# A batch's q and k through the DMA's transposition, and a new order of loads, in a fused attention and MLP kernel

## The chip, the cores and the metric

The kernel runs on one core of a Trainium2 chip. What counts is the device time of one execution in microseconds (us). Before the change the median of three runs is 226.33 us (226.27 to 227.69); the profiled execution spans 224.6 us, with TensorE's granted clock at 0.998.

A core has engines with an instruction queue each, worked off in order: TensorE (PE, matmuls; its weight loads are shown as PEld), VectorE (DVE), ScalarE (ACT), GpSimd (POOL) and SyncE (SP), which here only issues transfers. Transfers run on 16 DMA engines. Engines wait for each other, and for transfers, through semaphores. An instruction that waits holds back all that stand behind it on its engine.

## What is computed

Attention over a sliding window of 128 keys and four "sink" keys that all queries see, for 4 batches, 8 heads, 768 tokens and head size 64; then a layer norm and a two-layer MLP with a residual, on rows of 512:

```python
keep = (pos[None, :] < 4) | ((rel >= 0) & (rel < 128))        # rel = query - key
a = softmax(where(keep, q @ k.T / 8, -1e9))
x = (a @ v), heads side by side                                # (4, 768, 512)
xn = (x - mean) / sqrt(var + 1e-6) * g_ln
out = x + relu(xn @ w_ch1) @ w_ch2                             # 512 -> 2048 -> 512
```

Inputs and output are float32 in HBM; the matmuls run in bfloat16, and the loads issued by GpSimd change the type on the way.

## The kernel before

**Tiles.** A tile is 128 tokens of one batch: 24 tiles, six a batch (`RB`). For each tile `scores` (L545) multiplies k's block with 256 queries (its own and the next tile's) and takes the exponential on ScalarE; `values` (L617) multiplies with v, divides, takes the layer norm's statistics, and turns the normed rows so that the MLP can use them, on PE for tiles 0 to 9 and by a DMA transposition on SyncE from tile 10 (`DMA_TILE`). `sinks` handles the four sink keys of a batch and needs all its q blocks from token 256 on.

**MLP.** `up` (L731) computes hidden units of a group of tiles, `down` (L768) four of the sixteen hidden blocks (a "quarter") of one tile's output; the fourth quarter is followed by the residual and the store on SyncE. `GROUPS` is [2, 2, 2, 4, 4, 4, 4, 2]: the first three groups (`NB0`) are batch 0. Weights w1 and w2 come in four pieces of 512 KB (in bfloat16) each. `up` needs the piece of w1 for its hidden blocks, `down` the piece of w2 for its quarter; in the kernel before, quarters 0 and 1 wait for piece 2 (`w_in[(2, max(quarter, 2))]`).

**q and k.** Scores need q and k with the head dimension in the partitions. Three ways lead there. Batch 0 and batch 1 are loaded in long runs (`load_runs`, L346): batch 0 in two chunks of 384 tokens (the first four heads of chunk 0 by `load_first`), batch 1 whole, 768 KB each for q and k; `prep_runs` (L434) then turns them with PE transpositions (L454) and copies them out of PSUM on DVE and ACT (L222/L224). Batches 2 and 3 are loaded by token blocks of 128 KB (`load_qk`, L387), and `prep` (L470) turns each block with one DMA transposition issued by SyncE. `CHUNKS` tells which batches go which way.

**What sets the order.** Nothing is issued in the order in which the Python code calls it. Each piece of work is an `Op` with a cost for each engine that can do it, its dependencies and a due key; `Plan.emit` (L57) runs a list schedule over these and emits the instructions in the resulting order, one list for each engine. Costs and latencies are constants in the code: `LAT` by engine, the `took` of a load on one serial "DMA" resource, and for a DMA transposition an issue of 1.25 us on SP, 0.4 on a resource of its own ("XD") and 6.0 of extra latency (L481, L710). Up to `WARM` (26 us of the plan) the planner fills PE's gaps with `spin` matmuls (L236) of no use to the result. `HOLD` sets until when an operation of lower key may be taken ahead of a more urgent one's start. PSUM is two double banks ("wide", for scores and values) and four single banks ("single", for all else; the fourth holds the spin matmuls until the end of the warm-up).

**Loads.** All loads after the first few are issued by GpSimd (`load`, L328), in an order set by their keys, with up to eight under way: the ninth waits on the semaphore of the first. Before the change that order is: heads 4 to 7 of batch 0's chunk 0, v tiles 0 and 1, chunk 1 in four transfers, then w1 pieces and v tiles 2 to 5 in turn, three pieces of w2, batch 1's q and k, the last piece of w2, batch 1's v, batch 2's q and k. The lines that fix it are L822 to L841, and L869 to L877 for batches 1 to 3.

Of the kernel before, what the change touches and what calls it, by code (L numbers as in the profile page):

```python
# [11 lines left out]
ALU = mybir.AluOpType  # L12
# [19 lines left out]
class Plan:  # L32
# [10 lines left out]
    WARM = 26.0  # L43
    AHEAD = 2.5
    EARLY = 16.0
    HOLD = 22.0, 0.5

    def __init__(self, spin):
        self.ops, self.spin = [], spin
# [114 lines left out]
def kernel(  # L164
# [12 lines left out]
    nc = tc.nc  # L177

    B, H, S, D = q.shape
    NS = int(n_sink)  # L180
# [109 lines left out]
    def const_negs(_):  # L290
        nc.vector.tensor_scalar(neg1, mask1, 30000.0, -30000.0, op0=ALU.mult, op1=ALU.add)
        for m1, m0, keep in ((neg1, neg0, 0.0), (mask1, mask0, 1.0)):
            nc.vector.tensor_copy(m0, m1)
            nc.vector.memset(m0[0:NS, :], keep)

    def const_sinks(_):

        nc.gpsimd.affine_select(out=hmask[:, 0:1], in_=spinner[:, 0:1], compare_op=ALU.is_ge,
                                fill=0.0, base=63, pattern=[[0, 1]], channel_multiplier=-1)
        nc.gpsimd.affine_select(out=hmask[:, 1:2], in_=spinner[:, 0:1], compare_op=ALU.is_ge,  # L300
                                fill=0.0, base=-64, pattern=[[0, 1]], channel_multiplier=1)

        nc.gpsimd.affine_select(out=sel, in_=spinner, compare_op=ALU.is_equal, fill=0.0, base=0,
                                pattern=[[0, 32], [-1, NS]], channel_multiplier=1)

        nc.gpsimd.affine_select(out=smask, in_=spinner[:, 0:H], compare_op=ALU.is_ge, fill=0.0, base=0,
                                pattern=[[-32, HP], [-4, 2]], channel_multiplier=1)
        nc.gpsimd.affine_select(out=smask, in_=smask, compare_op=ALU.is_ge, fill=0.0, base=NS - 1,
                                pattern=[[32, HP], [4, 2]], channel_multiplier=-1)
# [7 lines left out]
    ident_done = op({"POOL": 0.35}, const_ident, [begun], -500)  # L317
    half_masks = op({"POOL": 0.6}, const_masks, [begun], -499.5)
    masks_done = neg_done = op({"DVE": 1.3}, const_negs, [half_masks], -700)
    sinks_done = op({"POOL": 1.4}, const_sinks, [begun], -440)  # L320

    QUEUE = 7
    issued, landed = [None], [None] * QUEUE

    def load(cost, took, go, key, deps=(), alloc=(), uses=()):  # L328
# [5 lines left out]

    CHUNKS = {0: 2, 1: 1}
    qn, loaded = {}, {}

    def qn_buf(b, x):  # L340
# [70 lines left out]
    w2s = consts.tile([128, NH1, DM], BF16)  # L411
    w_in = {}

    def load_w(which, c, key):
        def go(_):
            if which == 1:
                nc.gpsimd.dma_start(w1s[:, :, 512 * c:512 * (c + 1)],
                                    moe_w_ch1.rearrange("(j p) c -> p j c", p=128)[:, :, 512 * c:512 * (c + 1)])
            else:
                nc.gpsimd.dma_start(w2s[:, 4 * c:4 * (c + 1), :],  # L420
                                    moe_w_ch2.rearrange("(t p) n -> p t n", p=128)[:, 4 * c:4 * (c + 1), :])

        w_in[(which, c)] = load(0.85, 2.57, go, key)


    prepped, kqb, turns = {}, {}, {}
# [43 lines left out]
    def prep(b, x, r, lo, key):  # L470

        alloc = qkt_buf(b)
        kb, qb = kqb[b], qn[(b, x)]

        def go(_):
            if kb.t is None:
                kb.t = qkt.tile([128, 2, HP, S], BF16, name="qkt")
            nc.sync.dma_start_transpose(kb.t[:, x, :, 128 * r:128 * (r + 1)], qb.t[:, H * D * r:H * D * (r + 1)])

        o = op({"SP": 1.25}, go, [lo], key, alloc, [kb, qb])  # L480
        prepped[(b, r, x)] = op({"XD": 0.4}, None, [o], key, (), [kb, qb], 6.0)  # L481

    def ready(b, hps, klo, khi, qlo, qhi):

# [132 lines left out]
    def values(t, key):  # L617
# [89 lines left out]
        if t >= DMA_TILE:  # L707
            o = op({"SP": 1.25}, lambda _: nc.sync.dma_start_transpose(room(), xnb[t].t), [o], key, alloc,
                   [xnb[t], xtb[g]])
            turned[t] = op({"XD": 0.4}, None, [o], key, (), [xnb[t], xtb[g]], 6.0 if t < 18 else 0.0)  # L710
            return
        pt = Buf("pm", 0)

# [54 lines left out]
    def down(g, ti, quarter, c0, c1, key):  # L768

        t = FIRST[g] + ti  # L770
        n = c1 - c0
        alloc = []
        if quarter == 0:
            alloc = [Buf("pm", 0)]
            pcb[(g, ti, c0)] = alloc[0]
        pb = pcb[(g, ti, c0)]

        def mm(_):
            if quarter == 0:
                pb.t = room_for(pb)  # L780
            for ht in range(4 * quarter, 4 * quarter + 4):
                nc.tensor.matmul(pb.t[:, 0:n], lhsT=hidden(g, ht, ti), rhs=w2s[:, ht, c0:c1],  # L782
                                 start=(ht == 0), stop=(ht == NH1 - 1))

        hts = range(4 * quarter, 4 * quarter + 4)
        o = op({"PE": 0.865 * n / 512}, mm, [relu[(g, ht)] for ht in hts] + [w_in[(2, max(quarter, 2))], pre_down.get((g, ti))], key,
               alloc, [pb] + [h1b[(g, ht)][0] for ht in hts])
        pre_down[(g, ti)] = o
        if quarter == 3:
            b, r = divmod(t, RB)  # L790
            ob = Buf("ot", 3)
# [28 lines left out]
        nc.tensor.matmul(gp.t, lhsT=ones, rhs=grow, start=True, stop=True)  # L820

    for x in range(2):  # L822
        load_runs(0, 0, x, HP, H, (2.2, 1.1)[x], -499)
    for n, (x, hp) in enumerate((x, hp) for hp in range(2) for x in (1, 0)):
        load_first(x, hp, (3.3, 3.5, 4.6, 4.6)[n], -1000 + n)
    op({"SP": 0.1}, lambda _: nc.sync.dma_start(grow, moe_g_ln.rearrange("(o d) -> o d", o=1)), [], -900)
    for r in range(2):
        load_v(0, r, -496 + r, took=1.4)
    for half in range(2):
        for x in range(2):  # L830
            load_runs(0, 1, x, 4 * half, 4 * half + 4, ((1.5, 1.0), (1.8, 0.6))[half][x], -490 + 2 * half + x)
    for c in range(4):
        load_w(1, c, -470 + 2 * c)
        load_v(0, 2 + c, -469 + 2 * c)
    for c in range(3):
        load_w(2, c, -440 + c)
    for x in range(2):
        load_runs(1, 0, x, 0, H, 3.85, -436 + x)
    load_w(2, 3, -434)
    for r in range(RB):  # L840
        load_v(1, r, -430 + r)  # L841

    for b in range(B):
        k0 = bkey[b]
        if b == 0:
            for c in range(2):
                for hp in range(HP):
                    prep_runs(0, c, hp, k0 + (0.6 + 0.1 * hp if c else 0.05 if hp > 1 else -40))
                if c == 0:

                    gb_done = op({"PE": 1.0}, spread_g, [turns[(0, 0, 1)]], k0 - 1, [gp])
                    gb_done = op({"DVE": 0.65}, lambda e: copy(e, gb, gp.t), [gb_done], k0 + 0.32, (), [gp])
                    for n in range(4):
                        scores(n % 2, (n // 2,), k0 + 0.1 * n)
                    values(0, k0 + 0.4)
            sinks(0, akey(2) - 1)
            values(1, k0 + 0.5)
            for half in range(2):
                scores(2, (half,), akey(2))
            for r in range(3, RB):  # L860
                if r < RB - 1:
                    for half in range(2):
                        scores(r, (half,), akey(r))
                else:
                    scores(r, (0, 1), akey(r))
                values(r - 1, akey(r) - 0.5)
            values(RB - 1, akey(RB - 1) + 1.0)
            continue
        if b == 1:  # L869
            for hp in range(HP):  # L870
                prep_runs(1, 0, hp, k0 - 12 + 3 * hp)
        else:
            for r in range(RB):
                for x in range(2):
                    load_qk(b, x, r, k0 - 60 + r, [prepped.get((b - 1, RB - 1, 1))])
            for r in range(RB):
                load_v(b, r, k0 - 50 + r, [prepped[(b, RB - 1, 1)]])  # L877
        for r in range(RB):
            attention(RB * b + r, akey(RB * b + r))
            if r == 1:  # L880
                sinks(b, akey(RB * b + 2) - 1)

    for s, g in mlp_order:
# [5 lines left out]
                up(g, ht, up_pos[g] + 0.216 * GROUPS[g] * ht)  # L889
        else:  # L890
            at = down_pos[g]
            for ti in range(GROUPS[g]):

                for c0, c1 in ((0, 384), (384, DM)) if FIRST[g] + ti == NT - 1 else ((0, DM),):
                    for qu in range(4):
                        down(g, ti, qu, c0, c1, at)
                        at += 0.865 * (c1 - c0) / DM

    global TRACE
    TRACE = plan.emit()  # L900
# [35 lines left out]
```

## Time and profile before

| | us |
|---|---|
| median of three runs | 226.33 |
| span of the profiled execution | 224.6 |
| PE busy | 217.5 |
| POOL, ACT, DVE busy | 82.4, 111.1, 115.0 |
| first MLP1 block on PE (L742) starts | 21.21 |
| first MLP2 quarter (L782) starts | 52.19 |
| first scores of batch 2 (tile 12) start | 78.34 |

How to read the views: the page has busy time by engine, the span in 40 slices with a digit of busy tenths for each, the chain of waits that ended last, and groups of instructions. In the timeline each row is start, length, engine, line, operation with output and inputs, count, and in brackets the idle time before it with what ended it. In the view of one tile, a DMA row has issue times (ns) and when it was issued (us); the line "DMA to landing" counts from the issue to the moment at which all data has arrived, so issue plus that number is the landing. The matmul rows overlap by the pipeline's depth: pitch is read from start to start, not from lengths.

The chain of waits is on PE for 91% of the span: MLP2 (L782) 37%, MLP1 (L742) 36%, scores (L571) 5%. Of the DMA queues, q0 carries GpSimd's loads and q1 what SyncE issues, transpositions and output stores.

### The profile page before, as it was taken

What the parts mean: (1) busy time and instruction counts of PE and PEld (TensorE: products, weight loads), DVE (VectorE), ACT (ScalarE), POOL (GpSimd) and SP (SyncE); (2) the same over time, 40 slices, a digit from 0 to 9 for tenths busy, and PEclk for the clock granted to TensorE, in tenths of its full rate; (3) what the DMA queues carried; (4) which work ended last, traced back from release to release, by engine and by line L of the source; (5) the groups of instructions that cost most, each with busy time, mean ns of one, the idle gap of its engine ahead of it and who ended that gap; (6) DMA issues with size and microseconds to landing.
All of it is one profiled execution on the core that took longest, in us unless ns stands there. A gap on an engine that the chain in (4) does not pass through costs nothing.

```text
span 224.6 us, 4448 instructions
## 1 busy us (share of the span) xinstructions
PE 217.5 (97%) x1814; PEld 123.7 (55%) x1835; DVE 115.0 (51%) x217; ACT 111.1 (49%) x158; POOL 82.4 (37%) x111
## 2 busy tenths in 40 slices
PE   7999999999999999999999999999999999999994
PEld 6465888885545454455454444544454554444852
DVE  5565868044978879589574467470026750021011
ACT  3678775677342585870327762247613157400620
POOL 8978776669320699450733000220006020000000
PEclk9999999999999999999999999999999999999999
DMA  7999999999998599999799011230012130012102
GB/s 171 174 195 195 195 207 203 201 155 156 137 140 228 129 155 148 151 122 182 85 174 224 21 25 47 85 105 0 0 38 83 47 96 0 0 47 93 50 0 93
DMA packets 84774, 25.59 MB, mean 114 GB/s; under 512 B 74385, under 2 KB 81809, under 8 KB 84754
## 3 DMA queue, kind: packets, MB, share of 16 engines
q0 software_dynamic: 59392, 13.24, 67.9%
q1 hardware_dynamic: 24818, 11.67, 24.6%
q10 hardware_dynamic: 544, 0.39, 0.5%
q8 instruction: 14, 0.23, 0.4%
q14 instruction: 6, 0.05, 0.1%
HBM read 27.27 MB, written 6.29 MB: 149 GB/s over the span
## 4 chain that ended last, share of the span: by engine, by line
PE 91%; DVE 4%; DMA 2%; issue 1%; ACT 1%; DVEq 0%
PE single L782 37%; PE single L742 36%; PE wide L571 5%; PE wide L638 3%; PE wide L641 2%; PE wide L631 2%; DMA xnt<-in_q_dram 2%; PE wide L567 1%; PE wide L454 1%; PE single L718 1%; DVE st L671 1%; DVE xt L665 1%; PE single L236 1%; DVE xn L679 1%; PE single L454 1%
## 5 line engine op out<-in xcount | busy, mean ns | idle before, releaser
L742 PE MATMUL single<-xnt,w1s 128*128 128x256 bf16 (+1 forms) x503 | 87.1, 325 | 0.6 <-issue 0.2
L742 PEld LDWEIGHTS <-w1s 128*128 128x128 bf16 x512 | 48.4, 98 | 32.5 <-issue 1.9
L582 ACT ACTIVATE e<-wide 128x1024 bf16<-128x1024 f32 x44 | 43.6, 1023 | 43.4 <-PE wide L571 40.9
L782 PE MATMUL single<-w2s,h1t 128*128 128x512 bf16 x249 | 57.6, 379 | 0.4
L795 DVE SCALAR_TENSOR_TENSOR ot<-single,rs,xt 128x512 f32<-128x512 f32 (+2 forms) x25 | 18.2, 728 | 60.2 <-PE single L782 45.1
L751 ACT ACTIVATE h1t<-single 128x512 bf16<-128x512 f32 x60 | 35.8, 597 | 20.9 <-PE single L742 20.9
L782 PEld LDWEIGHTS <-h1t 128*128 128x128 bf16 x256 | 24.0, 98 | 28.1 <-issue 1.1
L782 PE MATMUL single<-w2s,h1n 128*128 128x512 bf16 (+2 forms) x139 | 29.6, 355 | 0.3
L751 ACT ACTIVATE h1n<-single 128x512 bf16<-128x512 f32 x30 | 17.9, 597 | 22.4 <-PE single L742 22.2
L594 POOL TENSOR_SCALAR_AFFINE_SELECT e<-e 128x512 bf16<-128x512 bf16 (+1 forms) x10 | 7.0, 701 | 47.8 <-ACT e L582 47.8
L691 POOL TENSOR_SCALAR ve<-mv 128x2 f32<-128x2 f32 (+1 forms) x8 | 5.7, 707 | 48.0 <-DVE mv L674 47.9
L404 POOL DMA_DIRECT2D vn<-in_v_dram x24 | 21.7, 922 | 0.0
L592 DVE TENSOR_TENSOR e<-e,mask 128x1024 bf16<-128x1024 bf16 x22 | 15.9, 722 | 9.4 <-ACT e L582 9.3
L782 PEld LDWEIGHTS <-h1n 128*128 128x128 bf16 x144 | 12.6, 98 | 12.3 <-issue 1.3
L679 DVE SCALAR_TENSOR_TENSOR xn<-xt,mv,gb 128x512 bf16<-128x512 bf16 x24 | 18.3, 768 | 0.7
L671 DVE BATCH_NORM_STATS2 st<-xt 128x6 f32<-128x512 bf16 x24 | 16.7, 694 | 0.8
L665 DVE TENSOR_TENSOR xt<-wide,rc 128x512 bf16<-128x512 f32 x24 | 16.6, 691 | 0.8
L638 PE MATMUL wide<-vn,e 128*128 128x65 bf16 x192 | 15.8, 193 | 0.1
L638 PEld LDWEIGHTS <-e 128*128 128x128 bf16 x192 | 13.7, 97 | 2.6 <-issue 0.2
L571 PE MATMUL wide<-qkt 64*128 64x256 bf16 (+1 forms) x192 | 14.5, 263 | 0.0
L641 PE MATMUL wide<-vn,e 128*128 128x65 bf16 x160 | 14.2, 193 | 0.0
L571 PEld LDWEIGHTS <-qkt 64*128 64x128 bf16 x192 | 6.7, 94 | 10.3 <-issue 9.3
(66 smaller groups left out, 166.1 us busy)
## 6 DMA issues: line engine op xcount, KB each, us to landing
out_dram<-ot SPq DMA_DIRECT2D x23, 256.0 KB, 2.2
vn<-in_v_dram POOLq DMA_DIRECT2D x24, 128.0 KB, 8.4
w1s<-in_moe_w_ch_dram POOLq DMA_DIRECT2D x4, 512.0 KB, 9.9
w2s<-in_moe_w_ch_dram POOLq DMA_DIRECT2D x4, 512.0 KB, 13.1
qkn<-in_q_dram POOLq DMA_DIRECT2D x12, 128.0 KB, 7.7
qkn<-in_k_dram POOLq DMA_DIRECT2D x12, 128.0 KB, 7.8
qkn<-in_q_dram POOLq DMA_DIRECT2D x1, 768.0 KB, 14.5
qkn<-in_k_dram POOLq DMA_DIRECT2D x1, 768.0 KB, 17.5
```

What stands on the lines that cost most here:

```text
L404: nc.gpsimd.dma_start(vn_buf[b % 2][:, r, :, 0:D], v[b, :, 128 * r:128 * (r + 1), :].rearrange("h p d -> p h d"))
L571: nc.tensor.matmul(pb.t[:, h2, i], lhsT=kb.t[64 * h2:64 * (h2 + 1), 1, hp, 128 * r:128 * (r + 1)], rhs=kb.t[64 * h2:64 * (h2 + 1), 0, hp, ...
L582: nc.scalar.activation(eb.t, pb.t, AF.Exp, scale=scale)
L638: nc.tensor.matmul(pv[:, half, hh, :], lhsT=weights_of(t, half, i, h2, 0), rhs=vn[:, r, h, 0:D + 1], start=fresh and hh == 0, stop=(r == 0 ...
L641: nc.tensor.matmul(pv[:, half, hh, :], lhsT=weights_of(t - 1, half, i, h2, 128), rhs=vn[:, r - 1, h, 0:D + 1], start=False, stop=True, ski ...
L665: nc.vector.tensor_tensor(xb[t].t.rearrange("p (a h) d -> p a h d", a=2), pv[:, :, :, 0:D], rc[0].unsqueeze(3).to_broadcast([128, 2, 4, D] ...
L671: nc.vector.bn_stats(st, xf)
L679: nc.vector.scalar_tensor_tensor(xnb[t].t, in0=xf, scalar=mvb[g][:, ti, 0:1], in1=gb, op0=ALU.subtract, op1=ALU.mult)
L742: nc.tensor.matmul(pb.t[:, n * i:n * (i + 1)], lhsT=w1s[:, j, 128 * (h0 + i):128 * (h0 + i + 1)], rhs=xtb[g].t[:, j, 0:n], start=(j == 0), ...
L751: nc.scalar.activation(hb.t, pb.t, AF.Relu)
L782: nc.tensor.matmul(pb.t[:, 0:n], lhsT=hidden(g, ht, ti), rhs=w2s[:, ht, c0:c1], start=(ht == 0), stop=(ht == NH1 - 1))
L795: nc.vector.scalar_tensor_tensor(ob.t[:, 0:n], in0=pb.t[:, 0:n], scalar=rsb[g][:, ti:ti + 1], in1=xb[t].t.rearrange("p h d -> p (h d)")[:, ...
```

## The change

Batch 1's q and k leave PE: they are loaded by token blocks like those of batches 2 and 3, and turned by DMA transpositions on SyncE. Their blocks are placed among the pieces of w1 and w2 and batch 1's v tiles. Each block can be used as soon as it is turned, so batch 1's attention is put earlier in PE's list, among batch 0's MLP1 blocks. Batch 0's MLP2 goes by quarters of w2 over three tiles at a time, so that it can begin with the first piece of w2; three single banks then hold sums at once. At the start, v tiles 0 and 1 go behind the first half of chunk 1, and the constant `sel` is made before the loads. Some of the planner's constants are new: a DMA transposition now takes 0.6 of the same serial "DMA" resource as the loads, with a latency of 2.0 - 0.5 (`TURN`); `HOLD` ends at 14; some `took` values differ. The purpose is to take 96 transpositions and the copies behind them off PE, DVE and ACT, and to use what is loaded sooner.

```diff
-    HOLD = 22.0, 0.5
+    HOLD = 14.0, 0.5
...
+    def const_sel(_):
+        nc.gpsimd.affine_select(out=sel, in_=spinner, compare_op=ALU.is_equal, fill=0.0, base=0,
+                                pattern=[[0, 32], [-1, NS]], channel_multiplier=1)
...
-        nc.gpsimd.affine_select(out=sel, in_=spinner, compare_op=ALU.is_equal, fill=0.0, base=0,
-                                pattern=[[0, 32], [-1, NS]], channel_multiplier=1)
...
+    op({"POOL": 0.5}, const_sel, [begun], -499.4)
...
+    TURN = -0.5
...
-    CHUNKS = {0: 2, 1: 1}
+    CHUNKS = {0: 2}
...
-        prepped[(b, r, x)] = op({"XD": 0.4}, None, [o], key, (), [kb, qb], 6.0)
+        prepped[(b, r, x)] = op({"DMA": 0.6}, None, [o], key, (), [kb, qb], TURN)
...
-            turned[t] = op({"XD": 0.4}, None, [o], key, (), [xnb[t], xtb[g]], 6.0 if t < 18 else 0.0)
+            turned[t] = op({"DMA": 0.6}, None, [o], key, (), [xnb[t], xtb[g]], TURN)
...
-        o = op({"PE": 0.865 * n / 512}, mm, [relu[(g, ht)] for ht in hts] + [w_in[(2, max(quarter, 2))], pre_down.get((g, ti))], key,
+        o = op({"PE": 0.865 * n / 512}, mm, [relu[(g, ht)] for ht in hts] + [w_in[(2, quarter)], pre_down.get((g, ti))], key,
...
-    for r in range(2):
-        load_v(0, r, -496 + r, took=1.4)
     for half in range(2):
         for x in range(2):
-            load_runs(0, 1, x, 4 * half, 4 * half + 4, ((1.5, 1.0), (1.8, 0.6))[half][x], -490 + 2 * half + x)
-    for c in range(4):
-        load_w(1, c, -470 + 2 * c)
-        load_v(0, 2 + c, -469 + 2 * c)
-    for c in range(3):
-        load_w(2, c, -440 + c)
-    for x in range(2):
-        load_runs(1, 0, x, 0, H, 3.85, -436 + x)
-    load_w(2, 3, -434)
-    for r in range(RB):
-        load_v(1, r, -430 + r)
+            load_runs(0, 1, x, 4 * half, 4 * half + 4, ((1.1, 1.0), (1.05, 2.1))[half][x], -498 + 2 * half + x)
+        if half == 0:
+            for r in range(2):
+                load_v(0, r, -496.5 + 0.1 * r)
+    order = [("w", 1, 0), ("v", 0, 2), ("w", 1, 1), ("v", 0, 3), ("w", 1, 2), ("v", 0, 4), ("v", 0, 5)]
+    order += [("b", 0), ("b", 1), ("w", 1, 3), ("b", 2), ("v", 1, 0), ("b", 3), ("v", 1, 1), ("w", 2, 0), ("b", 4), ("w", 2, 1),
+              ("b", 5), ("v", 1, 2), ("w", 2, 2), ("v", 1, 3), ("w", 2, 3), ("v", 1, 4), ("v", 1, 5)]
+    for n, (what, *at) in enumerate(order):
+        key = -470 + n
+        if what == "w":
+            load_w(*at, key, 2.6 if n else 2.25)
+        elif what == "v":
+            load_v(*at, key)
+        else:
+            for x in range(2):
+                load_qk(1, x, *at, key + 0.5 * x)
...
-        if b == 1:
-            for hp in range(HP):
-                prep_runs(1, 0, hp, k0 - 12 + 3 * hp)
-        else:
+        if b > 1:
...
+            if g < NB0:
+                continue
...
+    at = down_pos[0]
+    for n in range(0, RB, 3):
+        for qu in range(4):
+            for t in range(n, n + 3):
+                down(*where[t], qu, 0, DM, at)
+                at += 0.865
```

More of the change, by code (lines that the diff above doesn't have):

```diff
@@ L319 @@
     masks_done = neg_done = op({"DVE": 1.3}, const_negs, [half_masks], -700)
-    sinks_done = op({"POOL": 1.4}, const_sinks, [begun], -440)
+    op({"POOL": 0.5}, const_sel, [begun], -499.4)
+    sinks_done = op({"POOL": 0.9}, const_sinks, [begun], -440)
     QUEUE = 7
+    TURN = -0.5
     issued, landed = [None], [None] * QUEUE
@@ L412, with load_w @@
     w_in = {}
-    def load_w(which, c, key):
+    def load_w(which, c, key, took=2.6):
         def go(_):
@@ L421, in go @@
                                     moe_w_ch2.rearrange("(t p) n -> p t n", p=128)[:, 4 * c:4 * (c + 1), :])
-        w_in[(which, c)] = load(0.85, 2.57, go, key)
+        w_in[(which, c)] = load(0.85, took, go, key)
     prepped, kqb, turns = {}, {}, {}
@@ L822 @@
     for x in range(2):
-        load_runs(0, 0, x, HP, H, (2.2, 1.1)[x], -499)
+        load_runs(0, 0, x, HP, H, (2.1, 1.02)[x], -499)
     for n, (x, hp) in enumerate((x, hp) for hp in range(2) for x in (1, 0)):
-        load_first(x, hp, (3.3, 3.5, 4.6, 4.6)[n], -1000 + n)
+        load_first(x, hp, (3.75, 3.9, 4.75, 4.85)[n], -1000 + n)
     op({"SP": 0.1}, lambda _: nc.sync.dma_start(grow, moe_g_ln.rearrange("(o d) -> o d", o=1)), [], -900)
-    for r in range(2):
-        load_v(0, r, -496 + r, took=1.4)
     for half in range(2):
         for x in range(2):
-            load_runs(0, 1, x, 4 * half, 4 * half + 4, ((1.5, 1.0), (1.8, 0.6))[half][x], -490 + 2 * half + x)
-    for c in range(4):
-        load_w(1, c, -470 + 2 * c)
-        load_v(0, 2 + c, -469 + 2 * c)
-    for c in range(3):
-        load_w(2, c, -440 + c)
-    for x in range(2):
-        load_runs(1, 0, x, 0, H, 3.85, -436 + x)
-    load_w(2, 3, -434)
-    for r in range(RB):
-        load_v(1, r, -430 + r)
+            load_runs(0, 1, x, 4 * half, 4 * half + 4, ((1.1, 1.0), (1.05, 2.1))[half][x], -498 + 2 * half + x)
[14 more added lines that the diff above has]
+                load_qk(1, x, *at, key + 0.5 * x)
     for b in range(B):
```

## The prediction

> **What bounds the kernel now.** I read the page first: busy time of each engine, then the slices, then the chain of waits.
>
> ```profile
> PE 217.5 (97%) x1814; PEld 123.7 (55%) x1835; DVE 115.0 (51%) x217; ACT 111.1 (49%) x158; POOL 82.4 (37%) x111
> PE   7999999999999999999999999999999999999994
> DMA  7999999999998599999799011230012130012102
> ```
>
> TensorE is busy for 97% of the span. But the DMA engines stand at nine tenths in nearly every slice (5.6 us each) up to some 105 us: two resources are full in the first half, and only one of them is on the chain (PE 91%). So taking work from PE pays only if PE then waits for no transfer. The timeline of TensorE shows the work that goes, the first MLP1 block, and the first scores of batch 2:
>
> ```profile
> 21.21 1.05 PE L742 MATMUL single<-xnt,w1s 128*128 128x256 bf16 x8
> ...
> 45.39 1.53 PE L454 MATMUL wide<-ident,qkn 128*64 128x128 bf16 x48
> 46.85 1.05 PE L742 MATMUL single<-xnt,w1s 128*128 128x256 bf16 x8
> 48.13 1.73 PE L454 MATMUL wide<-ident,qkn 128*64 128x128 bf16 x48 [0.23 <-DVE qkt L224]
> 49.79 1.92 PE L742 MATMUL single<-xnt,w1s 128*128 128x256 bf16 x16
> ...
> 78.34 0.61 PE L571 MATMUL wide<-qkt 64*128 64x256 bf16 x8
> ```
>
> Read starts against starts: 46.85 - 45.39 = 1.46, 49.79 - 48.13 = 1.66, and 0.23 of idle.
>
> Then the transfers. The view of one tile in a narrow window gives one transfer's issue and its time to landing. Batch 2's first q block, the transposition of its q block 0, that of q block 1, and one late transposition with no loads queued:
>
> ```profile
> L395 POOL DMA_DIRECT2D qkn<-in_q_dram x1: 873/873/873, 43.6 to 43.6; - x1
> DMA to landing us min/median/max: 8.8/8.8/8.8
> ...
> L478 SPq DMA_TRANSPOSE qkt<-qkn x1: 1552/1552/1552, 52.4 to 52.4; - x1
> DMA to landing us min/median/max: 7.4/7.4/7.4
> ...
> L478 SPq DMA_TRANSPOSE qkt<-qkn x1: 1381/1381/1381, 55.3 to 55.3; - x1
> DMA to landing us min/median/max: 8.2/8.2/8.2
> ...
> L478 SPq DMA_TRANSPOSE qkt<-qkn x1: 1216/1216/1216, 71.8 to 71.8; - x1
> DMA to landing us min/median/max: 2.5/2.5/2.5
> ```
>
> Behind a full load queue a transposition takes 7.4 to 8.2 us, in a quiet one 2.5. Block q0 landed at 43.6 + 8.8 = 52.4, the transposition of q1 at 55.3 + 8.2 = 63.5: 11.1 us from the landing of q0 to the moment at which a tile's first scores (which need q0, k0 and q1) may start. Batch 3 gives the same from the same view: q0 issued at 81.6 landed after 5.5 (87.1), the transposition issued at 89.8 after 9.2 (99.0), so 11.9. Last, the DMA view with no transposition (50 to 52 us) and with both kinds (99 to 103 us):
>
> ```profile
> q0 software_dynamic: 2451, 0.31, 242.7%
> ...
> q0 software_dynamic: 2267, 0.28, 110.0%
> q1 hardware_dynamic: 1465, 0.35, 66.3%
> ```
>
> Alone the load queue moves 2451 packets in 2 us. Beside transpositions it moved 2267 in 4 us, which is 1.85 us of its own work; the other 2.15 went to 1465 packets. One transposition has 544 (the DMA view of a quiet stretch with a single one), so these are 2.7 of them: 0.8 us each.
>
> [...]
>
> **The change part by part.**
>
> *PE loses* 96 transpositions: 1.46 + 1.66 + 0.23 = 3.35 us of its path. The copies behind them (4 on DVE at 953 ns, 4 on ACT at 800 ns) lie beside PE work, so cost and gain nothing more.
>
> *The start* (v behind half of chunk 1, `const_sel` early, HOLD). `sel` costs 0.6 us on POOL before the first load (row L303, 597 ns). The loads of heads 4 to 7 landed at 7.7 at the latest and are used at 8.7; v0 and v1 move two places back, from 8.6 and 9.4 to about 11 and 12, and are used at 12.6 and 13.6: hidden. Chunk 1 arrives earlier, so PE's filler matmuls between 18.8 and 20.4 (13 of them) can shrink. Between 0 and 1.1 us; I take 0.6, first MLP1 block at 20.6.
>
> *MLP2 by quarters*: the same matmuls at the same 216 ns each. The old wait of quarter 0 for the third piece of w2 was over long before PE came (52.2 against 35.6). The new need, the last piece, is below.
>
> *Loads.* A whole-batch load took 3.8 us of queue (q and k landed at 39.4 and 43.3), a token block 0.9 (v: 40.1 + 10.5 = 50.5, 41.0 + 10.4 = 51.4). So 2 x 3.8 = 7.7 becomes 12 x 0.9 = 10.8: +3.1. Then 12 more transpositions on the same engines. Their cost: 0.6 if as in the quiet stretch (its DMA view has the engines busy for some six slices of 0.1 us), 1.2 if batch 3's whole stretch is taken (12 loads and 7 transpositions landed from 85.7 to 104.7: (19 - 10.8)/7). I take 0.9, so 10.8. SyncE gets 12 issues of 1.25 to 1.55 us; nothing was on it from 2 to 52 us, and what follows, stores and batch 2's transpositions, comes later anyway.
>
> *First new wait: tile 6.* The changed instruction order puts tile 6's scores after 9 MLP1 blocks (0.88 each, 7.9), three value groups (0.81, 2.4), four score groups (0.33, 1.3) and three transpositions of xn (0.22, 0.7): 12.3 us after the first block, at 32.9. The blocks are loaded after w1's third piece: v tile 4 landed at 24.5 before and stands at the same place now; then v5, and q0 of batch 1 lands at 26.4. With 11.2 more, q1 is transposed at 37.6. PE's queue is in order; all MLP1 blocks behind it wait too: 4.7 us.
>
> *Second: tile 12.* From v5 (25.5) the queue holds 12 blocks (10.8), four pieces of w2 and one of w1 (2.6 each, 13), six v (5.4), twelve transpositions (10.8): the last v of batch 1 lands at 65.5 (51.4 before). Batch 2's q0 follows at 66.4; 11.2 to q1's transposition, and two output stores now stand between on SyncE (0.54 each at issue): 78.6. When is PE there? The new order leaves six MLP2 quarters (0.865 each, 5.2) behind tile 12's scores and pulls 1.05 of batch-1 attention ahead: 4.15 earlier in the list. 78.34 - 3.35 - 0.6 - 4.15 = 70.2 without waits, 74.9 with the first. So 3.7 more: 8.4 us of waits in all. The last piece of w2 lands at 65.5 - 1.8 = 63.7; PE comes at 61.2 without waits, 65.9 with the first: hidden behind it. The remaining waits (batch 2's other blocks) come after 78.6 at PE's pace. After that the lists are alike up to the buffers.
>
> Sum: 226.33 - 3.35 - 0.6 + 8.4 = 230.8.
>
> **The rivals.**
>
> *A: no wait, 222.4.* If transpositions get turns between the packets of queued loads, as the planner's new figures assume (0.6 of transfer, 1.5 of latency), q1 is there at about 33 and PE does not stop: 226.33 - 3.35 - 0.6. For it: [...]the w pieces now in the stream have 1024-byte packets that leave more room than the 128-byte ones of the stretches I measured. Against: the 24 transpositions into qkt have a median of 7.0 us to landing (page, part 6) with the quiet ones counted in.
>
> *B: only tile 6 waits, 227.1.* If transpositions cost 0.6 of the queue, the last v comes 3.6 earlier and tile 12 is ready at 75.0, where PE arrives at 74.9. 222.4 + 4.7.
>
> *C: transpositions cost 1.2*: tile 12 at 82.2, waits 12.0, 234.4.
>
> **How the numbers follow.** Forecast 0.47, A 0.27, B 0.18, C 0.08. The time is the forecast's, 230.8. The range must reach into A, the only one on the other side, and up to C: 222.0 to 234.0 leaves out about the lower half of A's spread (0.12) and most of C (0.06). Faster by over 1% (below 224.1) is A, 0.27; within 1% is B, 0.18; slower (above 228.6) is the forecast and C, 0.55.
>
> **What would show it.** The changed timeline of PE should have the first scores of tile 6 behind an idle stretch of 3 to 6 us near 33 to 38, released by a DMA into qkt, and those of tile 12 behind another near 75 to 79. Batch 1's transpositions should take 7 us or more to land, its last v land at 63 to 68. The transposing matmuls (L454, L458 in the changed file) should number 96 less. It is wrong if those transpositions land within 4 us, or PE reaches tile 12 before 72, or if another wait (w2's last piece, the four single banks of PSUM, of which three now hold MLP2 sums) leads.

## The result, and the profile after

The changed kernel takes 243.17 us (median of four, 242.49 to 246.13) against 227.01 on the same chip: ratio 1.070, 95% interval 1.064 to 1.077. The profiled execution spans 241.8 us, 17.2 more than before. The page, in the lines that answer to those shown of before (busy time, slices, and the queue of GpSimd's loads):

```profile
PE 219.6 (91%) x1710; PEld 122.6 (51%) x1730; DVE 113.3 (47%) x213; ACT 107.7 (45%) x153; POOL 90.8 (38%) x122
PE   7999956992799919999999999999999999999995
PEclk9999997998599997999999999999999999999999
DMA  7999999999999999599999993123001231012102
...
q0 software_dynamic: 69792, 13.24, 82.4%
```

The same queue before:

```profile
q0 software_dynamic: 59392, 13.24, 67.9%
```

TensorE has 104 instructions fewer in the record and yet 2.1 us more of busy time. Three holes stand in its slices of 6.0 us (the sixth and seventh, the tenth and eleventh, the fifteenth), and the granted clock has a dip in or behind each. The DMA engines stand at nine tenths up to some 145 us, with one gap, instead of 105: the packets of the same 13.24 MB of loads take 82.4% of 16 engines' span instead of 67.9% of a shorter one. The view of waits says what TensorE stood for, the timeline when (start, length, then in brackets the idle time before):

```profile
PE wide L575 <- DMA qkt<-qkn: 15.5, 5, 5.9
```

```profile
33.99 0.40 PE L722 MATMUL single<-ident,xn 128*128 128x128 bf16 x4 [0.66 <-DVE xn L683]
38.62 1.04 PE L575 MATMUL wide<-qkt 64*128 64x256 bf16 x8 [4.24 <-DMA qkt<-qkn]
...
45.44 0.61 PE L575 MATMUL wide<-qkt 64*128 64x256 bf16 x8 [0.30 <-DMA qkt<-qkn]
...
62.00 1.03 PE L575 MATMUL wide<-qkt 64*128 64x256 bf16 x8 [5.93 <-DMA qkt<-qkn]
...
90.41 1.03 PE L575 MATMUL wide<-qkt 64*128 64x256 bf16 x8 [4.89 <-DMA qkt<-qkn]
```

These are the first scores of tiles 6, 7, 9 and 12; tile 8 waits another 0.15, and all 15.5 us are waits for a transposition. The rows at 38.62, 62.00 and 90.41 have 1.03 or 1.04 for eight matmuls, that at 45.44 has 0.61: the clock. The view by stretches, for TensorE alone (length, busy time and count, granted clock, DMA share, GB/s):

```profile
34.00:38.60 4.60, 0.39 (x4) 1.00 1.89 149
38.60:42.00 3.40, 3.38 (x20) 0.50 1.85 129
42.00:45.50 3.50, 3.20 (x42) 1.00 1.57 141
...
62.00:65.90 3.90, 3.90 (x24) 0.50 1.84 87
65.90:69.00 3.10, 3.05 (x18) 1.00 1.65 132
...
89.80:93.30 3.50, 2.89 (x13) 0.51 1.45 165
```

Nothing that stands behind the scores in TensorE's list ran ahead of them: the 4.60 us up to 38.60 hold 0.39 us of work. After each long wait TensorE works at half clock (0.50, 0.50 and 0.51): 3.4, 3.9 and 2.9 us of work at half speed lose, as an estimate, 1.7 + 1.95 + 1.45 = 5.1 us. The account is then 15.5 of waits + 5.1 of clock - 3.35 of transpositions - 1.0 of start (first MLP1 block at 20.19 instead of 21.21) = 16.25 of the 17.2 us; 0.95 is left without a name.

Last, the landings, from the view of one tile (issue time in the second group of numbers): the transposition of q1 that tile 6 waits for, one of block 5, and the last v of batch 1.

```profile
L482 SPq DMA_TRANSPOSE qkt<-qkn x1: 2072/2072/2072, 30.0 to 30.0; - x1
...
DMA to landing us min/median/max: 8.4/8.4/8.4
...
L482 SPq DMA_TRANSPOSE qkt<-qkn x1: 1330/1330/1330, 56.6 to 56.6; - x1
...
DMA to landing us min/median/max: 14.0/14.0/14.0
...
L408 POOL DMA_DIRECT2D vn<-in_v_dram x1: 873/873/873, 56.0 to 56.0; - x1
...
DMA to landing us min/median/max: 20.1/20.1/20.1
```

So q1 is turned at 38.5 and the last v lands at 76.1; before, the last v landed at 51.4.

### The profile page after: what moved, and what is told of

It reads as the page before. It is cut to its first block, busy times and chain, and to the rows that moved or that the text cites. A ratio compares the mean times of both kernels' runs of the same rounds, so it can differ in the third digit from the quotient of the medians.

```text
span 241.8 us, 4271 instructions
## 1 busy us (share of the span) xinstructions
PE 219.6 (91%) x1710; PEld 122.6 (51%) x1730; DVE 113.3 (47%) x213; ACT 107.7 (45%) x153; POOL 90.8 (38%) x122
## 3 DMA queue, kind: packets, MB, share of 16 engines
q0 software_dynamic: 69792, 13.24, 82.4%
## 4 chain that ended last, share of the span: by engine, by line
PE 72%; DMA 17%; POOL 4%; DVE 3%; ACT 2%; issue 2%; SPq 0%; DVEq 0%
PE single L786 33%; PE single L746 27%; DMA qkt<-qkn 8%; DMA qkn<-in_q_dram 8%; PE wide L575 4%; PE wide L642 2%; POOL qkn L399 1%; DMA xnt<-in_q_dram 1%; PE wide L645 1%; ACT e L586 1%; PE wide L635 1%; PE wide L571 1%; DVE ot L799 1%; PE single L458 1%; POOL vn L408 1%
## 5 line engine op out<-in xcount | busy, mean ns | idle before, releaser
L746 PE MATMUL single<-xnt,w1s 128*128 128x256 bf16 (+1 forms) x504 | 90.1, 332 | 0.4
L746 PEld LDWEIGHTS <-w1s 128*128 128x128 bf16 x512 | 49.7, 100 | 34.5 <-issue 2.6
L575 PE MATMUL wide<-qkt 64*128 64x256 bf16 (+1 forms) x192 | 15.8, 280 | 15.5 <-DMA qkt<-qkn 15.5
L598 POOL TENSOR_SCALAR_AFFINE_SELECT e<-e 128x512 bf16<-128x512 bf16 (+1 forms) x11 | 7.9, 721 | 55.8 <-ACT e L586 55.8
L755 ACT ACTIVATE h1n<-single 128x512 bf16<-128x512 f32 x28 | 16.7, 597 | 23.2 <-PE single L746 22.9
L683 DVE SCALAR_TENSOR_TENSOR xn<-xt,mv,gb 128x512 bf16<-128x512 bf16 x24 | 19.4, 810 | 0.8
L596 DVE TENSOR_TENSOR e<-e,mask 128x1024 bf16<-128x1024 bf16 x21 | 15.1, 721 | 10.1 <-ACT e L586 9.9
L695 POOL TENSOR_SCALAR ve<-mv 128x2 f32<-128x2 f32 (+1 forms) x8 | 4.2, 526 | 39.5 <-DVE mv L678 39.2
L399 POOL DMA_DIRECT2D qkn<-in_k_dram x18 | 16.0, 890 | 6.0 <-DMA w1s<-in_moe_w_ch_dram 1.6
L399 POOL DMA_DIRECT2D qkn<-in_q_dram x18 | 16.1, 896 | 5.3 <-DMA vn<-in_v_dram 4.7
L642 PE MATMUL wide<-vn,e 128*128 128x65 bf16 x192 | 15.8, 193 | 0.2
```

The source lines that it names most:

```text
L399: nc.gpsimd.dma_start(dst[:, r], (q, k)[x][b, :, 128 * r:128 * (r + 1), :].rearrange("h p d -> p h d"))
L575: nc.tensor.matmul(pb.t[:, h2, i], lhsT=kb.t[64 * h2:64 * (h2 + 1), 1, hp, 128 * r:128 * (r + 1)], rhs=kb.t[64 * h2:64 * (h2 + 1), 0, hp, ...
L642: nc.tensor.matmul(pv[:, half, hh, :], lhsT=weights_of(t, half, i, h2, 0), rhs=vn[:, r, h, 0:D + 1], start=fresh and hh == 0, stop=(r == 0 ...
L683: nc.vector.scalar_tensor_tensor(xnb[t].t, in0=xf, scalar=mvb[g][:, ti, 0:1], in1=gb, op0=ALU.subtract, op1=ALU.mult)
L746: nc.tensor.matmul(pb.t[:, n * i:n * (i + 1)], lhsT=w1s[:, j, 128 * (h0 + i):128 * (h0 + i + 1)], rhs=xtb[g].t[:, j, 0:n], start=(j == 0), ...
L755: nc.scalar.activation(hb.t, pb.t, AF.Relu)
```

## The experiments

Theory M, formed from this trace, is that the twelve transpositions among the queued loads cost the load queue far more than the 0.9 us each of the prediction, TensorE's in-order list meets their late arrival at tiles 6, 9 and 12, and each stall brings the half clock. Its rivals: R1, the smaller loads and their new order are the cost. R2, the other parts (MLP2 by quarters, the start) are. R3, the planner's latency is at fault, which puts the scores too early. R4, only the weight pieces beside them make transpositions dear.

**The change with batch 1's blocks turned on TensorE.** Same loads in the same order, no batch-1 transposition by DMA.

```diff
+        if b == 1:
+            loaded[(b, r, x)] = o
+            if x == 1:
+                prep_block(b, r, akey(RB * b + max(r - 1, 0)) - 3)
+            return
...
```

`prep_block`, left out here, holds 16 `nc.tensor.transpose` and two copies.

> The changed kernel with one thing undone: batch 1's token blocks are loaded as in the change, but each is turned by 16 transpositions on TensorE instead of two on the DMA (96 in all, 12 DMA transpositions fewer). Theory M (the 12 transpositions among the queued loads cost the load queue 1.7 us each, the scores of tiles 6, 9 and 12 wait for them in TensorE's in-order queue, and each stall is followed by 3.4 us at half clock): the last v of batch 1 lands near 76.1 - 12 x 1.7 = 55.4, no wait of more than 2 us before tiles 6, 9 and 12, about 226 to 229 us. R1 (the token blocks and their new place among the loads are the cost, not the transpositions): last v still lands after 70, 238 us or more. R2 (the other parts, MLP2 by quarters or the start, are the cost): 238 us or more, with the waits elsewhere.

227.18 us, ratio 1.0025 (1.0007 to 1.0042). The last v lands at 54.7, and no wait of TensorE is longer than the 1.1 us with which it starts. So 16 us hang on how the blocks are turned. R1 falls, and with it R2 as a main cause: loads, order, start and quarters are all in this kernel.

**The kernel before with the blocks and their DMA transpositions alone.**

```diff
-    CHUNKS = {0: 2, 1: 1}
+    CHUNKS = {0: 2}
...
-    for x in range(2):
-        load_runs(1, 0, x, 0, H, 3.85, -436 + x)
+    for r in range(RB):
+        for x in range(2):
+            load_qk(1, x, r, -436 + 0.2 * r + 0.1 * x)
...
-        if b == 1:
-            for hp in range(HP):
-                prep_runs(1, 0, hp, k0 - 12 + 3 * hp)
-        else:
+        if b > 1:
...
```

> The kernel before with one part of the change alone: batch 1's q and k by token blocks and DMA transpositions, in the place in the load order at which they stood (between the third and the fourth piece of w2), with the planner's old figures; start and MLP2 as before. M: 12 transpositions at 0.9 to 1.7 us and 3.1 us for the smaller loads move the last v from 51.4 to 65 to 75; TensorE waits for DMA into qkt at the first tiles of batch 1 and again at batch 2; 231 to 240 us. R1 (the new load order is the cost): 224 to 228 us, since the order is the old one. R2 (other parts): 223 us, which is 226.3 less the 3.35 us of transpositions on TensorE.

243.39 us, 1.070 (1.062 to 1.078): this part alone gives the whole loss, within M's range for the last v (68.2) and beyond it in time. But the waits are others:

```profile
PE single L782 <- DMA w2s<-in_moe_w_ch_dram: 4.8, 1, 4.8
PE single L742 <- DMA xnt<-xn: 3.5, 1, 3.5
PE single L530 <- DMA qkt<-qkn: 2.9, 2, 1.6
```

Here the last piece of w2 is late, since it stands behind the blocks. The queue lost less than in the changed kernel: from the third piece of w2 (37.04) to the last v 31.1 us passed, against 15.8 before plus 3.1 for the smaller loads, so 12.2 us for twelve, 1.0 each. The time lost is as large all the same. Which wait shows, and what it costs, depends on the order.

**The changed kernel with the planner's old figures for DMA transpositions.**

```diff
-        prepped[(b, r, x)] = op({"DMA": 0.6}, None, [o], key, (), [kb, qb], TURN)
+        prepped[(b, r, x)] = op({"XD": 0.4}, None, [o], key, (), [kb, qb], 6.0)
```

(and so for the transpositions of xn)

> The changed kernel with the planner's old figures for a DMA transposition (0.4 on its own resource and 6.0 of latency, instead of 0.6 of the load resource and 1.5). Loads, transpositions and their order stay; only the order in TensorE's list moves tile 6 and later scores back. R3 (the order is at fault: the scores stand too early in TensorE's list, the transfers themselves would do): 226 to 231 us, waits for DMA under 3 us. M (the transpositions take the load queue's time, so something late is always reached): last v of batch 1 still lands after 68, the waits move to other tiles or to w2's last pieces, 234 us or more.

250.9 us, 1.098 (1.090 to 1.106). R3 falls as far as these figures go: with more latency in the plan it is slower still. The last v lands at 75.9. The 5.25 us before the sinks of batch 1 (71.13) and 4.85 before a tile's scores (46.58) are the largest waits. A plan with the measured figures (1.8 us of the load queue, 7.6 to 14 us to land) was not tried, so how much a better order of TensorE's list would save is open.

**The size of it: six and six.** The text on record for the first of these two has the halves the wrong way round: the kernel that ran turned blocks 0 to 2 by DMA and 3 to 5 on TensorE. Against the kernel with all blocks on TensorE:

```diff
-        if b == 1:
+        if b == 1 and r >= 3:
```

> The changed kernel with the token blocks 0 to 2 of batch 1 turned on TensorE and the blocks 3 to 5 by DMA: 6 transpositions instead of 12 (none: 227.2 us, last v at 54.7; 12: 243.2 us, 76.1). M: in between, last v at 54.7 + 6 x (1.2 to 2.7) = 62 to 71, tile 6 waits no more, tile 9 or 12 does; 231 to 238 us. If only the first wait (tile 6) and what it drags along is the cost: 226 to 229 us. If only the last four transpositions are: 238 us or more.

231.7 us, 1.022 (1.018 to 1.026). Last v at 62.4, so (62.4 - 54.7)/6 = 1.28 us each. Tile 6 waits 4.62, as it needs q1. The other half, `r < 3` (blocks 3 to 5 by DMA):

> The changed kernel with blocks 0 to 2 of batch 1 turned on TensorE and blocks 3 to 5 by DMA. This is what was described for the earlier half run; that kernel had it the other way round (0 to 2 by DMA, 3 to 5 on TensorE: 231.7 us, last v at 62.4, 1.3 us for each of its six). If the place beside the pieces of w2 makes the last six dear: last v at 54.7 + 6 x 2.3 = 68.5, and 234 to 240 us. If their number does (twelve in a row, each standing behind others): 1.3 us each, last v near 62.4, and with tile 6 not waiting 228 to 232 us.

235.5 us, 1.036 (1.032 to 1.041). Last v at 67.5 in the traced execution, the longest of its four (237.5): 2.13 us each. The number is the same, so the place decides: 6 x 1.28 + 6 x 2.13 = 20.5, near the 21.4 us by which all twelve move the last v (76.1 - 54.7). The changed kernel once more:

> The changed kernel as it is, for a second trace. In the first, the eight transpositions of blocks 0 to 3 cost the load queue 1.3 us each and the four of blocks 4 and 5 2.7 us each (from 55.7 to 72.8 us, 6.2 us of loads). If that is the kernel's own: again 2 us or more for the last four, last v of batch 1 at 73 to 78. If it was an accident of one execution: 1.3 each, last v near 70.

243.0 us (one execution), last v at 74.9, (74.9 - 54.7)/12 = 1.68 each: the total is no accident of one execution. The dear stretch shifts: now the last four took 1.3 us each (56.7 to 71.6, with 9.7 us of loads landed), where the expectation had 2 or more, and the two of block 3 fell into the dear stretch, in which from 49.5 (first piece of w2) to 56.7 a single load of 0.9 us landed.

**All weights ahead of the blocks.** Transpositions then stand beside blocks and v, whose packets have 128 bytes (0.31 MB in 2451 packets from 50 to 52 us before); those of w1 and w2 have 1024 (1.22 MB in 1240 from 28 to 34 us, 38 of them under 512 bytes).

```diff
-    order = [("w", 1, 0), ("v", 0, 2), ("w", 1, 1), ("v", 0, 3), ("w", 1, 2), ("v", 0, 4), ("v", 0, 5)]
-    order += [("b", 0), ("b", 1), ("w", 1, 3), ("b", 2), ("v", 1, 0), ("b", 3), ("v", 1, 1), ("w", 2, 0), ("b", 4), ("w", 2, 1),
-              ("b", 5), ("v", 1, 2), ("w", 2, 2), ("v", 1, 3), ("w", 2, 3), ("v", 1, 4), ("v", 1, 5)]
+    order = [("w", 1, 0), ("v", 0, 2), ("w", 1, 1), ("v", 0, 3), ("w", 1, 2), ("v", 0, 4), ("v", 0, 5), ("w", 1, 3)]
+    order += [("w", 2, 0), ("w", 2, 1), ("w", 2, 2), ("w", 2, 3)]
+    order += [("b", 0), ("b", 1), ("b", 2), ("v", 1, 0), ("b", 3), ("v", 1, 1), ("b", 4), ("b", 5)]
+    order += [("v", 1, r) for r in range(2, RB)]
```

> The changed kernel with all pieces of w1 and w2 loaded ahead of batch 1's token blocks, so that the 12 transpositions stand beside 128-byte packets (blocks and v) and no 1024-byte weight pieces. M, with a transposition at 1.0 to 1.2 us in any company: from the last piece of w2 (near 40) to the last v 18 x 0.9 + 12 x 1.1 = 29 us, so 69; batch 1 starts later, but nothing of w2 is late; 232 to 240 us. R4 (only the weight pieces make transpositions dear, the 1.7 us mean of the changed kernel being theirs): 0.8 us each or less, last v by 66, each transposition lands within 8.5 us; 226 to 233 us.

Last v at 64.3: (64.3 - 54.7)/12 = 0.80 us each, and 6.4 to 8.5 us to land. That part is R4's, and M's "1.0 to 1.2 in any company" falls. The time is not R4's: 237.3 us, 1.048 (1.044 to 1.053), with 10 us of waits, since batch 1 now begins later (tile 6 at 50.2) and batch 2's sinks wait 5.7. So even at 0.80 the twelve transpositions in this order cost 10 us against the kernel that turns the blocks on TensorE (227.2).

The DMA view shows the kinds of company. First blocks and v beside transpositions in this kernel, 48 to 56 us; then the changed kernel from 42 to 50, with a piece of w2 and blocks in the stream (busy tenths in 40 slices of 0.2 us; packets and MB of loads, q0, and transpositions, q1):

```profile
DMA  9999999999999999999999999999999999999999
...
q0 software_dynamic: 4748, 0.60, 116.0%
q1 hardware_dynamic: 2602, 0.63, 62.8%
```

```profile
DMA  9999999999999999999999999999999999999999
...
q0 software_dynamic: 1994, 0.50, 90.3%
q1 hardware_dynamic: 1882, 0.46, 85.5%
```

Loads of 128-byte packets alone move at 155 GB/s (50 to 52 us before), pieces of w2 alone at 207 (28 to 34 us before). At these rates the loads of the first window need 3.9 of its 8 us, which leaves 0.9 for each of its 4.8 transpositions; those of the second need 2.4 to 3.2, which leaves 1.4 to 1.6 for each of its 3.5. These are estimates; the landings give 0.80, and 1.3 for the first eight of the changed kernel (q4 landed at 51.95, 25.7 us after the last v of batch 0, of which loads take 15.1). Last the changed kernel from 64 to 72, with two pieces of w2:

```profile
DMA  5991119999999999999965599949980119999999
GB/s 60 68 28 28 23 26 76 77 81 80 84 177 180 142 128 120 160 141 134 133 79 95 83 135 218 108 51 40 29 15 7 10 17 166 159 150 140 120 124 115
DMA packets 2292, 0.76 MB, mean 95 GB/s; under 512 B 1880, under 2 KB 2291, under 8 KB 2291
```

In the same 8 us 0.76 MB pass, where the first window had 1.23. Twice the engines stand under two tenths for 0.6 us (slices 4 to 6 and 31 to 33, down to 7 GB/s) with loads and transpositions under way. Of the 2292 packets 27 take over 1 us, up to 1.7; in the two windows above none takes over 0.8. Such a stall isn't peculiar to weight pieces. The kernel before has one too, from 96.5 to 97.6 us (window 94 to 100, slices of 0.15 us), with three transpositions and loads of 128-byte packets alone under way:

```profile
DMA  9999999999999999940111118999999999999999
GB/s 160 154 159 157 150 143 152 159 159 163 255 152 145 132 149 96 40 8 3 8 10 9 9 9 78 137 153 158 156 160 156 160 159 160 145 146 157 158 160 155
```

So two things make the price: a lower rate beside weight pieces (119 GB/s from 42 to 50 us, where the first window has 154), and single stalls of 0.6 to 1.1 us, beside weight pieces and beside narrow loads. What holds the packets in a stall is not shown.

**Idle transpositions in the kernel before.** Four more, of data that nobody reads, beside the weight pieces (one execution each, here and in the next run):

```diff
+    for n in range(4):
+        op({"SP": 1.25}, lambda _, n=n: nc.sync.dma_start_transpose(
+            w2s[:, 12 + n, :].rearrange("p (t r) -> p t r", t=NDM), w1s[:, 0, 0:512]), [w_in[(1, 0)]], -469 + 0.1 * n)
```

> The kernel before with four DMA transpositions more, each of 128 x 512 as those of the token blocks, issued when the first piece of w1 has landed, of data that nobody reads; nothing waits for them but the last piece of w2, some 14 us later. So they stand among the pieces of w1 and w2 and the v tiles. M at 1.7 us each: they land 7 to 12 us after their issue and every later load comes 6.9 us later (third piece of w2 at 42.5 instead of 35.6, last v at 58.3 instead of 51.4). At the 0.9 us of the prediction: 3.6 us later (55.0). If transpositions fill gaps between packets of loads: less than 1 us, landing after 2.5 to 4 us.

228.7 us. The third piece of w2 landed at 40.62 instead of 35.59; 0.23 of that was there in the v tile ahead of them: 4.8/4 = 1.2 us each, between the two values expected. The same four after the third piece of w2, beside k in packets of 768 bytes (0.80 MB in 1037 from 38 to 42 us before), and, as it came out, the last piece of w2 and the first v:

> The kernel before with four DMA transpositions more, of data that nobody reads, as in the kernel whose four stood among the 1024-byte packets of w1 and w2 (1.2 us each there), but issued after the third piece of w2 has landed (35.6), beside the whole-batch loads of q and k, whose packets are of 768 bytes. R4 in a packet-by-packet form (the wider the packets that take turns with it, the dearer a transposition: 0.8 us beside 128 bytes, 1.2 beside 1024): about 1.1 us each, last v at 55.8 instead of 51.4. If only company with weight pieces matters: 0.8 each, 54.6. If it is a fixed price: 1.2 each, 56.2. In all cases the time stays within 2 us of the kernel before.

230.2 us, last v at 57.4; less the 0.43 of earlier shift 5.5/4 = 1.4 us each, above all three values. The time is beyond the 2 us too, with 1.8 of a wait for a mask on GpSimd at 62.8. So wide company is dearer than narrow (1.2 and 1.4 against 0.8), but not in proportion to its packets. The width is not taken apart from the rest: weight pieces are also four times as large as a block.

**The other parts.** The change without its part on batch 1:

> The changed kernel without the part on batch 1: q and k of batch 1 by long runs and TensorE transpositions in their old place of the load order and with the planner's old figures for DMA transpositions; what is left of the change is the start (v behind half of chunk 1, sel early, the hold), and MLP2 of batch 0 by quarters over three tiles. M and R1: within 2 us of the kernel before, 224 to 228. R2: 235 us or more.

230.2 us, 1.015 (1.010 to 1.020): the parts said to gain 0.6 us cost 3.6, between M's and R2's figures. Taken apart, the start alone (v tiles 0 and 1 behind half of chunk 1, `const_sel`, `HOLD` 14.0):

> The kernel before with the start of the change alone (v behind half of chunk 1, sel early, the shorter hold); batch 1 and MLP2 as before. The prediction's step: first MLP1 block 0.6 us earlier, 225.9 us. If the start is what brought 3.6 us in the kernel with both other parts (a group's xn transposition arriving late near 118 us): 229 to 231 us.

225.84 us, 0.9970 (0.9956 to 0.9984): 0.75 us faster than before, the one version that beats both kernels. And the quarters alone (`w_in[(2, quarter)]`, three tiles at a time):

> The kernel before with batch 0's MLP2 by quarters of w2 over three tiles alone. The prediction's step: same matmuls, nothing hidden or exposed, 226 to 227 us. If the quarters are what brought the 3.6 us: 229 to 231 us.

229.1 us, 1.011 (1.009 to 1.014). Its timeline shows why:

```profile
118.59 1.02 PE L742 MATMUL single<-xnt,w1s 128*128 128x512 bf16 x3 [2.55 <-DMA xnt<-xn]
```

An MLP1 block 66 us after the first quarters meets a transposition of normed rows that lands at 118.5. SyncE's list has the reason: its rows for these transpositions, first of the kernel before, then with the quarters:

```profile
106.28 4.91 SPq L708 DMA_TRANSPOSE xnt<-xn  x3
```

```profile
110.45 2.54 SPq L708 DMA_TRANSPOSE xnt<-xn  x2
...
113.66 2.94 SPq L708 DMA_TRANSPOSE xnt<-xn  x2
```

Both stand behind the twelve transpositions of batch 3's q and k, which begin at 87.18 before and at 90.22 here. The third one, for which the block waits, is issued at 113.66 instead of 109.97; before, it had landed at 114.59, and MLP1 began at 115.80 without a wait. Why batch 3's come later is open. A larger latency in the plan was to move the block back (against the kernel of the other parts):

```diff
-            turned[t] = op({"XD": 0.4}, None, [o], key, (), [xnb[t], xtb[g]], 6.0 if t < 18 else 0.0)
+            turned[t] = op({"XD": 0.4}, None, [o], key, (), [xnb[t], xtb[g]], 9.0 if t < 18 else 0.0)
```

> The kernel with the start and the quarters, and in the planner 9.0 instead of 6.0 of latency for the transpositions of normed rows by DMA, so that the MLP1 block that waited 2.8 us for one of them near 118 us stands later in TensorE's list. If that wait and the 1 us at a lower clock behind it are the whole 3.6 us: 225 to 227 us, and with the start's gain perhaps just below the kernel before. If the wait moves to another place: 229 us or more.

230.1 us, 1.015 (1.011 to 1.018): the same wait, 2.4 us at 118.7. The planner's figure does not reach it.

Whether the quarters cost also in the new load order was put to two runs. The changed kernel without quarters:

> The changed kernel with MLP2 of batch 0 tile by tile as before, waiting for the third piece of w2. If the quarters cost 2.5 us here as in the kernel before: 240 to 241 us. If they pay here, since they let MLP2 begin with the first piece of w2 in a stretch in which TensorE lacks work: 245 us or more. If neither: 243.

Inconclusive: four executions gave 235.6, 243.3, 248.1 and 249.9 us from the same instructions. In the fastest, the only one traced, a transposition cost (68.9 - 55.0)/12 = 1.2 us (55.0 is the last v of the next kernel) and no scores after tile 6 waited over 0.4 us; batch 1's sinks waited 4.85. The change with blocks on TensorE and without quarters:

> The changed kernel with batch 1's blocks turned on TensorE and MLP2 tile by tile: what is left of the change is the start and the loads by token blocks in their new order. If the quarters cost 2.5 us here too: 227.2 - 2.5 = 224.7 us, faster than the kernel before by 0.8%. If the quarters cost nothing in this order (no wait of TensorE was seen in it): 227 us. If MLP2 now waits for the third piece of w2, which lands at 49.6 here instead of 35.6: 228 us or more.

229.4 us, 1.013 (1.009 to 1.018): 2.2 us slower than with quarters, the time of the expectation's third case, but not by its reason: its trace shows no wait for w2, only one long wait of 1.8 us at 120.5, for a residual on VectorE (L827). In the load order of before quarters cost 2.5 us, in the new one they pay 2.2; why they pay is not shown.

## Why the prediction was right and wrong

Right: the direction, by the reason given. *PE loses* 96 transpositions, and L458 shows 96 fewer. *The start* held: 0.6 predicted, 0.75 alone. *First new wait*: TensorE stood at 34.4 (32.9 predicted), q1 was turned at 38.5 (37.6), the wait was 4.24 (4.7). Batch-1 transpositions took 7.6 us or more, over the 7 named. Rival A, a free ride between the packets, is gone.

Wrong: the term "I take 0.9, so 10.8". In its place stood 21.4 us for twelve, 1.78 each. The window of 99 to 103 us from which 0.8 came has only 128-byte packets beside the transpositions, and there it is right: the run with all weights ahead gives 0.80. But the new order puts them among 1024-byte pieces, and there 1.2 to 2.1 was measured. I noted these packets under rival A, as leaving "more room", which no trace had shown; the sign was the other way. With 1.78 in the step's own sum, 65.5 + 12 x 0.88 = 76.1, which is what the trace has; and without the term the sum has 54.7, which is what the kernel without these transpositions has. Rival C's end of 1.2 was too near because batch 3's stretch, too, has no weight pieces. That stretch did hold a stall, at 96.5; the narrow window began just behind it.

What followed from it: the two waits forecast came out near their sum, 4.24 + 4.89 = 9.1 against 8.4, but by luck: tile 12 was ready at 90.3 instead of 78.6, and TensorE was itself late and came at 85.5 instead of 74.9. The largest wait, 5.93 us, is tile 9's, which the prediction did not follow; that another wait leads was one of its own signs of being wrong. Its q4 stands behind 15.1 us of loads after v5 (11 blocks and v tiles at 0.9, two weight pieces at 2.6) and eight transpositions. With 0.9 for these, q4 lands at 26.3 + 15.1 + 7.2 = 48.6 and is turned 8.2 later, 56.8, when TensorE comes at 56.1; measured were 51.95 and 61.87. So the mis-sized term makes most of this wait, in the queue and again in the 9.9 us that the transposition itself took. The price alone is not the whole, though: at 1.0 each, in the old order, the loss was 16 us, and at 0.80, with all weights ahead, still 10.

Missing altogether, put at nothing: the half clock after a stall, 5.1 us. Of the 12.75 us by which the spans' difference (17.2) exceeds the forecast's (4.45), 7.1 are more waits and 5.1 the clock. The trace has 0.50 or 0.51 in stretches of 3.4 to 3.9 us at the ends of the waits of 4.24, 5.93 and 4.89. Behind shorter waits the half clock came or did not. The run with blocks 3 to 5 by DMA has both cases (the stretch behind a wait of 1.88 us, then one inside a wait of 3.38, then the stretch behind that; the columns as above):

```profile
46.00:49.40 3.40, 3.40 (x30) 0.50 3.36 128
51.30:54.60 3.30, 0.00 (x0) 1.00 1.63 118
54.70:58.10 3.40, 3.40 (x39) 1.00 1.57 133
```

The first stretch stands behind the wait of 1.88, which ended at 44.93, and has the half clock; the wait of 3.38, in the second row, had none in it or behind it. Near 118.5, too, a wait of 2.79 (the kernel of the other parts) was followed by 3.5 us at 0.52, one of 2.42 (the larger latency in the plan) by six MLP1 matmuls in 2.65 us where 33 later ones take 7.50, and one of 2.55 (quarters alone) by 3.4 us at 1.00. So the length of these doesn't decide, and what does is not shown. Every wait of 3.39 us or more in these traces was followed by the half clock: 0.50 to 0.64 in the nine stretches of 3.3 to 3.9 us that were read at the ends of such waits.

The step "*MLP2 by quarters*: the same matmuls" was right for the matmuls and wrong for the order: 2.5 us in the kernel before, through a wait far behind. For the changed kernel itself it is open what they cost.

Beside narrow loads a transposition was as fast as a load, 0.80 us of the load queue for 128 KB against 0.9 for a block's load; beside weight pieces, at 1.2 to 2.1, it was not.

## What to carry to other kernels

Measure the price of a transfer in the company in which it will run, and over a stretch long enough to hold its stalls: a transposition cost 0.8 to 1.0 us of the load queue beside mostly 128-byte packets and 1.2 to 2.1 with wide ones in the stream, and twelve of them made 3.35 us of saved TensorE work into a loss of 16. On an in-order engine follow the late transfers to every instruction that needs them, not to the first and the last, and count the half clock behind a stall as well: here it followed every stall of 3.39 us or more (2.9 to 3.9 us of work at 0.50 or 0.51 in the changed kernel) and three of the five shorter ones named above. A reordering costs where its effect surfaces, which may be 60 us later, so run each part alone: here the only gain, 0.3%, lay in the smallest one.

## What was not expected of the hardware

Transpositions and loads don't merely share the engines: now and then both stand nearly still with work under way (0.6 to 1.1 us in the windows shown, at 3 to 28 GB/s), beside weight pieces and beside narrow loads alike. A stretch with such stalls does not keep its place: in the first trace of the changed kernel the dear one begins at 56, in the second at 49.5. One thing stands ahead of some of them: a single packet on the queue of instructions (q8), at 95.57 in the kernel before and at 68.81 ahead of the second stall of the changed kernel. None stands between 57.5 and the first stall at 64.6, so this is at most part of the cause; no run takes it apart.

The changed kernel without quarters ran from 235.6 to 249.9 us with the same instructions, where every other kernel stayed within 2.2% of its fastest. As only its fastest execution was traced, what the others met is not known.
